# Heads paired four apart, whole batches of k and v in one tile, and chunks 6 to 11 worked by halves of 64 tokens

## The chip, the cores and the metric

The kernel runs on one core of one Trainium2 chip. The metric is the device time of one execution in microseconds. Before the change three runs gave 214.65, 214.87 and 215.19 us, a median of 214.87. One execution was profiled; it took 214.73 us.

## What is computed

A retention layer and a feed-forward layer, in float32 at the interface and bf16 on the way:

```python
gamma = 1 - 2.0 ** (-5 - h)                      # one per head h
state = gamma * state + outer(k[t], v[t])        # per batch and head, 64 x 64
y[t]  = q[t] @ state / sqrt(64)
x     = y, heads side by side: (4 * 768, 8 * 64)
out   = relu(x @ w_in) ** 2 @ w_out              # 512 -> 2048 -> 512
```

There are 4 batches, 8 heads, 768 tokens each, heads of 64. q, k and v are 6.3 MB each, w_in and w_out 4.2 MB each, the output 6.3 MB.

## The kernel before

**Chunks.** Tokens are taken in 24 chunks of 128 (six to a batch). Within a chunk the recurrence is a masked product: scores k q, times powers of gamma that are put into q and k beforehand, times a mask, times v; the state of the chunks before comes in as one more product. Chunks 0 to 3 (`PAIRED`) are worked two at a time by functions named `..._pair`. Chunks 4 to 11 go 128 tokens at a time with `attend`: `scale_q`, `scale_kv`, a transpose of q and k (on TensorE for chunks 4 to 7, by DMA from chunk 8 on, `DMA_FROM`), `scores`, `state`, `outputs`. Chunks 12 to 23 (`PACK_FROM`) go with `attend2` by two halves of 64 tokens: `scale_k2`, `cast_v2`, `transpose_k2` (by DMA), `scores2`, `state2` for each half, `outputs2`. In that form two heads share the 128 rows of a weight load, one on rows 0 to 63 and one on rows 64 to 127, which is why `cast_v2` writes a block-diagonal copy of v beside the plain one.

**Feed-forward.** `BLOCKS` puts four chunks into the first token block and two into each of the other ten. `ffn_pieces` cuts a block's two products into pieces of about 0.87 us of TensorE, eight to a chunk. After every piece a counter `n` goes up by one and `before(n)` issues what `put(place, ...)` has hung on that place: loads, scalings, transposes, scores, outputs. So all order is written by hand in places; place 32 is the end of the first block, and each later block has sixteen. Each engine works off its own instructions in that order.

**Heads and rows.** Heads 2p and 2p+1 make pair p; the 512 columns of x are in the order of the heads, and w_in is loaded in that order: 128 rows by 4 blocks.

**Loads.** All transfers are issued by SP, on one queue: loads, output stores and the transposes by DMA. Each waits until the transfer eight before it has landed, and, where its tile is used again, for those who read it. Weights are staged in a ring of five tiles of 1 MB, then cast to bf16 (`cast_w`, `cast_w_out`). k and v come by chunk (`load`) for chunks 4 to 11, in loads of 256 KB. For chunks 12 to 23 they come by threes (`group_loads`): per head one load of 96 KB into 64 rows, so sixteen loads for three chunks of k and v.

The lines of the profile are: L777 first product, L835 second product, L786 relu, L757 square, L367 and L380 transposes of q and k on TensorE, L421, L447, L476 and L484 scores, state and the two kinds of output matmuls of `attend`, L681, L708, L730 and L737 the same of `attend2`, L717 and L718 copies of the state, L744 the copy of the outputs, L353 `scale_kv`'s cast of v, L656 and L659 `cast_v2`, L643 `scale_k2`, L334 `scale_q`, L847 the stores.

Of the kernel before, what the change touches and what calls it, by code (L numbers as in the profile page):

```python
# [9 lines left out]
FP32 = mybir.dt.float32  # L10
# [9 lines left out]
LDBUFS = 4  # L20
# [4 lines left out]
DMA_FROM = 8  # L25


PACK_FROM = 12

GROUP = 3  # L30
# [3 lines left out]
def kernel(  # L34
# [9 lines left out]
    nc = tc.nc  # L44
# [22 lines left out]
    ldpool = ctx.enter_context(tc.tile_pool(name="ldpool", bufs=LDBUFS // 2))  # L67
    grpool = ctx.enter_context(tc.tile_pool(name="grpool", bufs=2))
    qspool = ctx.enter_context(tc.tile_pool(name="qspool", bufs=2))
    kspool = ctx.enter_context(tc.tile_pool(name="kspool", bufs=4))  # L70
# [6 lines left out]
    wstage = ctx.enter_context(tc.tile_pool(name="wstage", bufs=5))  # L77
# [43 lines left out]
    def group_loads(m):  # L121

        b, i = chunks[m]
        for name, src, to in (("kg", k, raw_k), ("vg", v, raw_v)):
            t = grpool.tile([P, 2 * GROUP, NPAIR, D], FP32, name=name)
            for h in range(H):
                p, hh = divmod(h, 2)
                rows = slice(64 * hh, 64 * (hh + 1))
                nc.sync.dma_start(
                    t[rows, :, p, :],  # L130
                    src[b, h, i * C : (i + GROUP) * C, :].rearrange("(w s) d -> s w d", s=64),
                )
                yield
            for j in range(GROUP):
                to[m + j] = t[:, 2 * j : 2 * j + 2].rearrange("s u p d -> s (u p) d")

    w_in_v = moe_w_in.rearrange("(cb p) f -> p cb f", p=P)
# [3 lines left out]
    def load_w_in(g, parts=1):  # L141
        t = wstage.tile([P, NCB, FQ], FP32, name="w_stage")
        n = FQ // parts
        for j in range(parts):
            nc.sync.dma_start(
                t[:, :, j * n : (j + 1) * n], w_in_v[:, :, g * FQ + j * n : g * FQ + (j + 1) * n]
            )
        staged["in", g] = t

    def load_w_out(g):  # L150
        t = wstage.tile([P, FPQ, DM], FP32, name="w_stage")
        nc.sync.dma_start(t[:], w_out_v[:, g * FPQ : (g + 1) * FPQ, :])
        staged["out", g] = t
# [16 lines left out]
    halves = [slice(0, 64), slice(64, 128)]  # L170
# [66 lines left out]
    def pack_constants():  # L237
        lng2 = const.tile([P, 2, NPAIR], FP32)
        for hh, rows in enumerate(halves):
            for p in range(NPAIR):  # L240
                nc.gpsimd.memset(lng2[rows, :, p : p + 1], float(np.log(gammas[2 * p + hh])))
        logs = lng2.rearrange("s u p -> s (u p)")
        ex = exponents([[C, NCH], [C // 2, 2], [0, NPAIR]], 1, "ex_k2", logs, halves)
        nc.scalar.activation(kf2.rearrange("s i u p -> s i (u p)"), ex[:], AF.Exp, scale=-1.0)
        nc.gpsimd.memset(cmask2[:], 0.0)
        for rows in halves:
            nc.gpsimd.affine_select(
                out=cmask2[rows],
                in_=cmask2[rows],
                compare_op=ALU.is_gt,  # L250
                fill=1.0,
                base=0,
                pattern=[[-1, 2], [-2, C // 4]],
                channel_multiplier=1,
            )
# [75 lines left out]
    def scale_q(m):  # L331
        b, i = chunks[m]
        qs = qspool.tile([P, 2, H, D], BF16, name="qs")
        nc.vector.tensor_tensor(  # L334
            out=qs[:],
            in0=raw_q.pop(m).rearrange("s h r d -> s r h d"),
            in1=qf[:, i : i + 2, :, None].to_broadcast([P, 2, H, D]),
            op=ALU.mult,
        )
        at[m]["qs"] = qs  # L340

    def scale_kv(m):
        b, i = chunks[m]
        ks = kspool.tile([P, H, D], BF16, name="ks")
        nc.vector.tensor_tensor(
            out=ks[:],
            in0=raw_k.pop(m)[:],
            in1=kf[:, i, :, None].to_broadcast([P, H, D]),
            op=ALU.mult,
        )  # L350
        v_bd = v_bds[m % 2]
        vn = raw_v.pop(m)
        nc.gpsimd.tensor_copy(  # L353
            v_bd[:, :, ::3, :], vn.rearrange("s (p hh) d -> s p hh d", hh=2)
        )
        at[m].update(ks=ks, v_bd=v_bd)
# [40 lines left out]

    def dma_transpose_k(m):
        a = at[m]
        kT = kTpool.tile([P, 2 * NPAIR, C], BF16, name="kT")  # L400
        nc.sync.dma_start_transpose(kT[:, 0:NPAIR], a["ks"].rearrange("s h d -> s (h d)"))
        a["kT"] = kT

    def spread_k(m):
        a = at[m]
        kT = a.pop("kT")
        k_bd = k_bds[m % 2]
        for hh in range(2):
            rows = slice(64 * hh, 64 * (hh + 1))
            nc.vector.tensor_copy(k_bd[rows, :, hh, :], kT[rows, 0:NPAIR])  # L410
        a["k_bd"] = k_bd
# [91 lines left out]
    def scale_pair_q(m, r, engine=nc.vector):  # L503
        b, i = chunks[m]
        if r == 0:
            at[m]["qs"] = qspool.tile([P, 2, H, D], BF16, name="qs")
        engine.tensor_tensor(
            out=at[m]["qs"][:, r],
            in0=raw_q[m].rearrange("s h r d -> s r h d")[:, r],
            in1=qf[:, i + r, :, None].to_broadcast([P, H, D]),  # L510
            op=ALU.mult,
        )

    def scale_pair_k(m, r):
        b, i = chunks[m]
        at[m]["ks"] = pair_view(ks_bd2s[m // 2])
        nc.vector.tensor_tensor(
            out=at[m]["ks"][:, r],
            in0=raw_k[m][:, r],
            in1=kfp[:, i + r, :, None].to_broadcast([P, H, D]),  # L520
            op=ALU.mult,
        )
# [54 lines left out]
    def state_pair(m, j):  # L577
# [5 lines left out]
        for p in range(NPAIR):  # L583
            for r in range(2):
                nc.tensor.matmul(  # L585
                    c[:, p],
                    lhsT=a["ks"][halves[j], r, 2 * p : 2 * p + 2, :],
                    rhs=a["v"][halves[j], r, 2 * p : 2 * p + 2, :],
                    start=(i + j == 0 and p == 0 and r == 0),
                    stop=True,  # L590
                    skip_group_check=True,
                )
# [4 lines left out]
    def outputs_pair(m, r, pools=None):  # L597
# [4 lines left out]
        for p in range(NPAIR):  # L602
            for hh, head in enumerate(halves):
                for j, rows in enumerate(halves):
                    nc.tensor.matmul(
                        a["y"][j][head, p, :],
                        lhsT=a["v"][rows, r, 2 * p + hh, :],
# [30 lines left out]
    def scale_k2(m):  # L638
# [3 lines left out]
        for hh, rows in enumerate(halves):  # L642
            nc.vector.tensor_tensor(  # L643
                out=ks[rows, :, hh, :],
                in0=kn[rows],
                in1=kf2[rows, i].rearrange("s u p -> s (u p)")[:, :, None].to_broadcast(
                    [64, 2 * NPAIR, D]
                ),
# [4 lines left out]
    def cast_v2(m):  # L653
        vn = raw_v.pop(m)
        v2 = v2pool.tile([P, 2 * NPAIR, D], BF16, name="v2")
        nc.gpsimd.tensor_copy(v2[:], vn[:])  # L656
        v_bd = v_bd2s[m % 2]
        for hh, rows in enumerate(halves):
            nc.gpsimd.tensor_copy(v_bd[rows, :, hh, :], vn[rows])  # L659
# [211 lines left out]
    scale_pair_q(0, 0)  # L871
    scale_pair_q(0, 1)
# [8 lines left out]
    scale_pair_q(2, 0, nc.gpsimd)  # L881
    scale_pair_q(2, 1, nc.gpsimd)
# [50 lines left out]
    def attend_q(m, scaled, transposed):  # L933
        if m % 2 == 0:
            put(scaled, scale_q, m)
            put(transposed, dma_transpose_q if m >= DMA_FROM else transpose_q, m)

# [3 lines left out]
    def attend(m, scaled, places):  # L941
        by_dma = m >= DMA_FROM
        attend_q(m, scaled, scaled if by_dma else places[0])
        put(places[0], scale_kv, m)
        if by_dma:
            put(places[0], dma_transpose_k, m)
        put(places[1], spread_k if by_dma else transpose_k, m)
# [5 lines left out]
    def attend2(m, d):  # L953
        attend_q(m, d - 17, d - 15)
        put(d - 15, scale_k2, m)
        put(d - 15, cast_v2, m)
        put(d - 13, transpose_k2, m)
        put(d - 6, state2, m, 0)
# [6 lines left out]
    for m, place in ((5, 10), (6, 14), (7, 18)):  # L965
        put(place, load, m)
# [7 lines left out]
    attend(6, 30, (33, 35, 37, 39, 42))  # L974
    attend(7, None, (40, 42, 44, 46, 49))
    put(50, pack_constants)
    for j, t in enumerate([s_bds[2]] + ks_bd2s + v_bd2s):
        for hh in range(2):
            put(51 + 3 * j + hh, zero_off_diagonal, t, hh)


    done = [55, 62, 70] + [78 + 8 * j for j in range(13)]
    for m, place in ((8, 29), (9, 31), (10, 36)):
        put(place, load, m)
    for m, d in zip(range(8, NCHUNK), done):
        if m < PACK_FROM:
            attend(m, d - 15 if d < 70 else d - 16, (d - 13, d - 7, d - 5, d - 3, d))
        else:
            attend2(m, d)
        if m + 3 < PACK_FROM:  # L990
            put(d - 13, load, m + 3)
        elif m + 3 < NCHUNK and (m + 3) % 2 == 0:
            put(d - 13, load_q, m + 3)
    for m, place in zip(range(PACK_FROM, NCHUNK, GROUP), (43, 67, 92, 116)):
        loads = group_loads(m)
        for j in range(2 * H):
            put(place + 3 * j // 2, next, loads)
        put(place + 3 * H, next, loads, None)
# [43 lines left out]
```

## Time and profile before

| what | value |
|---|---|
| median of three runs | 214.87 us |
| profiled execution | 214.73 us |
| its span, first to last instruction | 212.9 us |
| TensorE busy | 204.5 us, 96% |
| VectorE, ScalarE, POOL busy | 61%, 55%, 24% |
| bytes moved | 39.65 MB, mean 186 GB/s |
| SP's queue, share of 16 transfer engines | 79.4% |
| granted TensorE clock, mean | 0.992 |

The page divides the span into 40 slices and gives the busy share of each engine in tenths for each. The chain follows the work that ended last back to the start: who held up whom. In a table of stretches, the numbers behind an engine's name are its busy time and instructions in that stretch; the last three columns are the granted TensorE clock, the busy share of the sixteen transfer engines (it can pass 1, because transfers overlap) and the bytes moved per time. Times of SP's instructions are the time that SP spent on issuing; it grows where the queue is full.

### The profile page before, as it was taken

To read this page: it belongs to the slowest core of one execution; us is meant where nothing else is said; L and a number is where in the kernel's file an instruction comes from. 1 tells how busy PE (TensorE), PEld (TensorE's weight loads), DVE (VectorE), ACT (ScalarE), POOL (GpSimd) and SP (SyncE) were. 2 spreads that over 40 slices of the span, in tenths; PEclk is the share of its full clock that TensorE was granted. 3 is DMA by queue.
4 is the path that set the end of the run, shared out by engine and by line. 5 is a ranking of instruction groups with operands and counts; after the bars stand their busy time and mean duration, and the time that the engine had idled before them with its cause. 6 is when DMAs were issued, how large, how long until landed. Compare 5 with 4: busy or idle time off the path is not lost.

```text
span 212.9 us, 5128 instructions
## 1 busy us (share of the span) xinstructions
PE 204.5 (96%) x2077; PEld 142.1 (67%) x2077; DVE 129.4 (61%) x257; ACT 116.2 (55%) x216; POOL 50.6 (24%) x106
## 2 busy tenths in 40 slices
PE   5789999999999999999999999999999999999994
PEld 1467644558966975875875875875965965965853
DVE  4777875265585696796495595593694693640410
ACT  8365885358853643652663663652753754643631
POOL 5332466221110411025121323008122223000000
PEclk9889999999999999999999999999999999999999
DMA  6999999999969898599698698998795452401102
GB/s 162 290 317 383 386 386 258 293 242 274 276 172 201 199 197 145 161 207 182 164 197 191 154 189 188 152 194 202 164 240 127 99 80 72 102 0 49 52 0 99
DMA packets 90551, 39.65 MB, mean 186 GB/s; under 512 B 66336, under 2 KB 84000, under 8 KB 90528
## 3 DMA queue, kind: packets, MB, share of 16 engines
q1 hardware_dynamic: 90528, 39.33, 79.4%
q8 instruction: 16, 0.26, 0.6%
q14 instruction: 7, 0.06, 0.1%
HBM read 27.26 MB, written 6.29 MB: 158 GB/s over the span
## 4 chain that ended last, share of the span: by engine, by line
PE 90%; ACT 2%; DVE 2%; DMA 2%; POOL 1%; issue 1%; POOLq 0%; ACTq 0%; DVEq 0%
PE psf L835 38%; PE psf L777 38%; DMA qn<-in_q_dram 2%; PE st L421 2%; PE y L484 1%; PE st L681 1%; PE y L737 1%; PE y L730 1%; PE c_ps L708 1%; PE y L313 1%; DVE pt L568 1%; PE c_ps L585 1%; PE psf L544 1%; ACT osb L845 1%; PE c_ps L447 1%
## 5 line engine op out<-in xcount | busy, mean ns | idle before, releaser
L777 PE MATMUL psf<-xt,w_in_bf 128*128 128x256 bf16 (+2 forms) x880 | 90.7, 259 | 0.2 <-ACT xt L492 0.2
L835 PE MATMUL psf<-w_out_bf,h 128*128 128x512 bf16 (+2 forms) x400 | 89.6, 371 | 0.0
L777 PEld LDWEIGHTS <-w_in_bf 128*128 128x128 bf16 x880 | 71.3, 98 | 11.8 <-issue 0.3
L786 ACT ACTIVATE h<-psf 128x512 bf16<-128x512 f32 x96 | 57.0, 597 | 22.2 <-PE psf L777 19.6
L835 PEld LDWEIGHTS <-h 128*128 128x128 bf16 x400 | 36.3, 98 | 35.1
L757 DVE TENSOR_TENSOR h<-h 128x512 bf16<-128x512 bf16 x96 | 43.1, 467 | 21.0 <-ACT h L786 20.2
L845 ACT ACTIVATE osb<-psf 128x512 f32<-128x512 f32 (+2 forms) x25 | 14.5, 580 | 28.6 <-PE psf L835 28.6
L718 DVE CAST s_bd<-c_ps 64x256 bf16<-64x256 f32 x22 | 9.4, 427 | 27.4 <-ACT s_bd L717 27.1
L656 POOL CAST v<-vg 128x512 bf16<-128x512 f32 x12 | 8.1, 674 | 56.3 <-PE c_ps L708 21.0
L659 POOL CAST v_bd<-vg 64x512 bf16<-64x512 f32 x24 | 16.4, 682 | 15.0 <-PE y L737 14.1
L428 DVE TENSOR_TENSOR pt<-st,cmask 128x512 bf16<-128x512 f32 x16 | 11.1, 692 | 12.5 <-PE st L421 12.3
L643 DVE TENSOR_TENSOR ks_bdp<-kg,kf 64x512 bf16<-64x512 f32 x24 | 18.3, 762 | 0.4
L353 POOL CAST v_bd<-vn 128x512 bf16<-128x512 f32 x8 | 5.7, 718 | 36.2 <-PE y L484 29.1
L744 ACT ACTIVATE xt<-y 128x512 bf16<-128x512 f32 x12 | 8.9, 742 | 9.6 <-PE y L737 9.6
L334 DVE TENSOR_TENSOR qs<-qn,qf 128x1024 bf16<-128x1024 f32 x10 | 12.1, 1213 | 2.1 <-DMA qn<-in_q_dram 2.0
L717 ACT ACTIVATE s_bd<-c_ps 64x256 bf16<-64x256 f32 x22 | 8.1, 367 | 8.8 <-PE c_ps L708 8.8
L301 POOL CAST w_out_bf<-w_stage 128x512 bf16<-128x512 f32 x12 | 7.8, 689 | 5.5 <-DMA w_stage<-in_moe_w_out_dram 5.5
L492 ACT ACTIVATE xt<-y 128x512 bf16<-128x512 f32 x8 | 6.0, 749 | 5.5 <-PE y L484 5.2
L688 DVE TENSOR_TENSOR pt<-st,cmask 128x512 bf16<-128x512 f32 x12 | 8.3, 691 | 0.4
L313 PE MATMUL y<-ident 128*128 128x512 bf16 (+1 forms) x13 | 5.8, 558 | 2.1 <-POOL ident L199 2.1
L708 PEld LDWEIGHTS <-ks_bdp 128*128 128x128 bf16 x88 | 5.6, 98 | 2.6
L737 PE MATMUL y<-pt,v_bd 128*128 128x64 bf16 x96 | 7.0, 193 | 0.0
(99 smaller groups left out, 167.1 us busy)
## 6 DMA issues: line engine op xcount, KB each, us to landing
qn<-in_q_dram SPq DMA_DIRECT2D x12, 512.0 KB, 4.9
out_dram<-osb SPq DMA_DIRECT2D x23, 256.0 KB, 2.5
w_stage<-in_moe_w_out_dram SPq DMA_DIRECT2D x4, 1024.0 KB, 12.2
w_stage<-in_moe_w_in_dram SPq DMA_DIRECT2D x3, 1024.0 KB, 11.8
kg<-in_k_dram SPq DMA_DIRECT2D x32, 96.0 KB, 3.6
vg<-in_v_dram SPq DMA_DIRECT2D x32, 96.0 KB, 3.4
kn<-in_k_dram SPq DMA_DIRECT2D x8, 256.0 KB, 5.6
vn<-in_v_dram SPq DMA_DIRECT2D x8, 256.0 KB, 5.6
```

Of the source, the lines that this page charges most:

```text
L334: nc.vector.tensor_tensor(out=qs[:], in0=raw_q.pop(m).rearrange("s h r d -> s r h d"), in1=qf[:, i : i + 2, :, None].to_broadcast([P, 2, H ...
L428: nc.vector.tensor_tensor(out=a["pt"][:, 2 * half : 2 * half + 2], in0=st[:], in1=cmask.rearrange("s r t -> s (r t)")[:, None, None, :].to ...
L643: nc.vector.tensor_tensor(out=ks[rows, :, hh, :], in0=kn[rows], in1=kf2[rows, i].rearrange("s u p -> s (u p)")[:, :, None].to_broadcast([6 ...
L659: nc.gpsimd.tensor_copy(v_bd[rows, :, hh, :], vn[rows])
L718: nc.vector.tensor_copy(s_bd[halves[1], :, 1, :], c[halves[1]])
L737: nc.tensor.matmul(yv, lhsT=a["v_bd"][:, u * NPAIR + p], rhs=a["pt"][:, u * NPAIR + p, :].rearrange("s (r t) -> s r t", r=2), start=not inter,
L744: nc.scalar.activation(xts[tb][:, :, off : off + C].rearrange("e p (s r) -> e p r s", r=2), y[:], AF.Copy,)
L757: nc.vector.tensor_mul(hv, hv, hv)
L777: nc.tensor.matmul(hp, lhsT=w_in_bf[g][:, cb, fq * 128 : (fq + 1) * 128], rhs=xts[tb][:, cb, cols], start=(cb == 0), stop=(cb == NCB - 1),)
L786: nc.scalar.activation(hv, hp[:], AF.Relu)
L835: nc.tensor.matmul(op[:], lhsT=h_of(tb, f)[:, 0, j * C : (j + 1) * C], rhs=w_out_bf[g][:, fq, cols], start=(f == 0), stop=(f == NFB - 1),)
L845: nc.scalar.activation(osb[:, cols], op[:], AF.Copy)
```

## The change

1. **Pairing.** Pair p is now heads p and p + 4. Scalings go through one helper, `scale`, that reads in the loaded order and writes in pair order; `cast_v2`, `scale_k2` and the products of the paired chunks take the heads accordingly. Rows of w_in are in pair order, and each `load_w_in` is cut into one load per pair. `scale_q` becomes two instructions of one token parity each.
2. **Staging.** One ring of four tiles of 1.5 MB (`stage`) holds weights and whole batches of k or v, in place of the ring of five and the tiles of `group_loads`.
3. **Whole loads.** `load_batch` loads k or v of a whole batch with two loads of 786 KB into 64 rows each: for chunks 8, 12 and 18. The first of them is of batch 1, so it holds chunks 6 and 7 too, which are not taken from it.
4. **Own loads.** k and v of chunks 6 and 7 come by `load_two`, eight loads of 64 KB each, hung on places 13 to 18.
5. **Halves from chunk 6 on.** `PACK_FROM` goes from 12 to 6, so chunks 6 to 11 go with `attend2`, with outputs at places 47, 52, 59, 63, 70, 78 (before: 42, 49, 55, 62, 70, 78). q of chunk 6 and k of 6 and 7 are now transposed by DMA; k transposes of 8 to 11 grow to two halves. Constants and cleared blocks for the halves are made at places 14 to 24 instead of 50 to 64.

On SP the order is now: the first six loads, 20 loads of w_in, w_out 0 to 2, chunk 4, w_out 3, chunk 5, q of 6, the sixteen own loads, the first block's stores with q of 8 among them, the transposes of q and k of 6, k of batch 1, the transpose of k of 7, v of batch 1, q of 10, the transpose of q of 8, two stores, the transposes of k of 8 and 9. w_out 0 takes the tile of w_in 0, so it waits for the casts of that; before it had a tile of its own.

```diff
-PACK_FROM = 12
+PACK_FROM = 6
-    kspool = ctx.enter_context(tc.tile_pool(name="kspool", bufs=4))
+    kspool = ctx.enter_context(tc.tile_pool(name="kspool", bufs=2))
-    wstage = ctx.enter_context(tc.tile_pool(name="wstage", bufs=5))
+    stage = ctx.enter_context(tc.tile_pool(name="stage", bufs=4))
...
+    def load_two(m, name):
+        b, i = chunks[m]
+        src, to = (k, raw_k) if name == "k" else (v, raw_v)
+        t = ldpool.tile([P, 2 * H * D], FP32, name=name + "n")
+        t = t.rearrange("s (w p d) -> s w p d", w=4, p=NPAIR)
+        for w in range(4):
+            t0 = i * C + w * 64
+            for hh, rows in enumerate(halves):
+                nc.sync.dma_start(t[rows, w],
+                    src[b, NPAIR * hh : NPAIR * (hh + 1), t0 : t0 + 64].rearrange("p s d -> s p d"))
+                yield
...
+    def load_batch(m, name):
...
+        for hh, rows in enumerate(halves):
+            nc.sync.dma_start(
+                t[rows].rearrange("s p w d -> s (p w) d"),
+                src[b, NPAIR * hh : NPAIR * (hh + 1)].rearrange("p (w s) d -> s (p w) d", s=64),
+            )
...
-    w_in_v = moe_w_in.rearrange("(cb p) f -> p cb f", p=P)
+    w_in_v = moe_w_in.rearrange("(hh p d) f -> p hh d f", hh=2, d=D)
...
-            nc.sync.dma_start(
-                t[:, :, j * n : (j + 1) * n], w_in_v[:, :, g * FQ + j * n : g * FQ + (j + 1) * n]
-            )
+            for p in range(NPAIR):
+                nc.sync.dma_start(
+                    t[:, p, j * n : (j + 1) * n],
+                    w_in_v[p, :, :, g * FQ + j * n : g * FQ + (j + 1) * n],
+                )
...
+    def scale(engine, out, by, table):
+        engine.tensor_tensor(
+            out=out.rearrange("s (p hh) d -> s hh p d", hh=2),
+            in0=by.rearrange("s (hh p) d -> s hh p d", hh=2),
+            in1=table.rearrange("s (hh p) -> s hh p", hh=2)[:, :, :, None].to_broadcast([P, 2, NPAIR, D]),
+            op=ALU.mult,
+        )
...
-    for m, place in ((5, 10), (6, 14), (7, 18)):
-        put(place, load, m)
+    put(10, load, 5)
+    put(13, load_q, 6)
+    for name, place in (("k", 13), ("v", 16)):
+        loads = load_two(6, name)
+        for j in range(9):
+            put(place + j // 3, next, loads, None)
...
-    attend(6, 30, (33, 35, 37, 39, 42))
-    attend(7, None, (40, 42, 44, 46, 49))
-    put(50, pack_constants)
+    put(14, pack_constants)
...
+    done = [47, 52, 59, 63] + [70 + 8 * j for j in range(14)]
+    ahead = {6: (34, 35, 39), 7: (37, 38, 44), 8: (48, 49, 50), 9: (53, 54, 55), 10: (60, 61, 60)}
+    for m, d in zip(range(PACK_FROM, NCHUNK), done):
+        attend2(m, d, done[m - PACK_FROM - 1] if m > PACK_FROM else 0,
+                d - 17 if m < 8 else d - 18, *ahead.get(m, (d - 15, d - 13, d - 15)))
+    for m, name, place in (
+        (8, "k", 36), (8, "v", 39), (12, "k", 62), (12, "v", 66), (18, "k", 98), (18, "v", 106)
+    ):
+        put(place, load_batch, m, name)
```

`attend2` now takes the places of the scaling and the transpose of k and of the cast of v (the three numbers in `ahead`) as arguments.

## The prediction

> **What bounds the kernel now.** I read the page's first four parts, then stretches of the trace, then SP's issues in order of time.
>
> ```profile
> span 212.9 us, 5128 instructions
> PE 204.5 (96%) x2077; PEld 142.1 (67%) x2077; DVE 129.4 (61%) x257; ACT 116.2 (55%) x216; POOL 50.6 (24%) x106
> PE   5789999999999999999999999999999999999994
> DMA  6999999999969898599698698998795452401102
> PE 90%; ACT 2%; DVE 2%; DMA 2%; POOL 1%; issue 1%; POOLq 0%; ACTq 0%; DVEq 0%
> ```
>
> TensorE holds the chain: 90% of it, busy in every slice after the third. What idles it is the start; later only 0.27 us at 72 to 74. But the transfer engines are full from the second slice to the eleventh and are never far from it until the thirtieth. So TensorE's work sets the time only as long as the queue delivers in time, and the queue has little to spare.
>
> How fast it delivers, by stretches (the last two columns are the busy share of 16 transfer engines and GB/s):
>
> ```profile
> 8.00:12.00 4.00, 3.77 (x48) 2.23 (x47) 3.13 (x7) 1.75 (x3) 2.04 (x2) 0.58 1.22 290
> 14.00:17.00 3.00, 2.71 (x61) 2.05 (x62) 1.55 (x4) 2.58 (x6) 1.91 (x4) 1.00 1.11 360
> 22.00:29.00 7.00, 7.00 (x48) 3.68 (x46) 5.87 (x19) 5.45 (x12) 2.71 (x7) 1.00 1.05 386
> 45.80:49.00 3.20, 3.20 (x30) 1.98 (x28) 2.33 (x3) 2.72 (x6) 0.29 (x1) 1.00 1.35 221
> ```
>
> Rows of 512 bytes go at 290 GB/s, of 1 KB at 360, of 2 KB at 386, of 256 bytes (k and v) at 221. All sixteen engines share each load here: per engine 22.5 GB/s for 1 KB rows (360/16) and 24.1 for 2 KB (386/16).
>
> When SP issued (start, us spent):
>
> ```profile
> 6.68 1.74 SPq L102 DMA_DIRECT2D vn<-in_v_dram  x1
> 8.46 5.78 SPq L145 DMA_DIRECT2D w_stage<-in_moe_w_in_dram  x5
> 38.00 3.38 SPq L94 DMA_DIRECT2D qn<-in_q_dram  x1
> 45.34 1.01 SPq L113 DMA_DIRECT2D vn<-in_v_dram  x1
> ```
>
> Landings keep the order of issue throughout. The vn issued at 6.68 takes 7.3 us and lands at 14.0; the last w_in load, issued at 13.15, takes 13.3 and lands at 26.5; the vn of chunk 7 (45.34) takes 4.9 and lands at 50.2.
>
> **What it removes.** From the chain in order of time:
>
> ```profile
> 39.45 0.45 PE tp L367 x8
> 41.62 0.22 PE tp L380 x4
> 45.52 0.22 PE st L421 x4
> 45.74 0.22 PE c_ps L447 x4
> 101.93 0.12 PE c_ps L708 x4
> 102.92 0.23 PE st L681 x8
> ```
>
> A chunk of the old kind costs 2 x 0.22 (scores), 0.22 (state) and twelve output matmuls, 53.21 to 53.88, 0.67: 1.33. By halves: 0.23, 2 x 0.12 and sixteen output matmuls, 115.21 to 115.68, 0.47: 0.94. Four chunks save 0.39 each; chunk 6 (first of its batch) and chunk 11 (last) 0.3 each. Three transposes leave TensorE: q of chunk 6 (0.45), k of 6 and 7 (0.22 each). With the 0.27 us wait behind the constants, which are now made earlier, TensorE is relieved of 1.56 + 0.6 + 0.89 + 0.27 = 3.3 us.
>
> **New order on TensorE.** Chunk 7's outputs move to place 52, and the next piece reads them through ACT: 0.74 (L744) plus handover, 0.9 us idle (0.7 to 1.3). State of chunk 9 is formed twice with one piece between; its two copies (0.37 and 0.43) just fill that: 0.3 (0 to 1).
>
> **Costed at nothing.** VectorE: the split q scaling (two of 0.69 for one of 1.21, ten pairs, 1.7 us) and the clearing and constants moved to places 14 to 24 lie in its idle 39%. POOL: the casts of six more chunks (three of 0.68 in place of one of 0.72) lie in its idle 76%; without that cover each would delay an output by 1.3 us. The w_out 0 load now waits on SP for the casts of w_in 0, with w_out 1, w_out 2 and chunk 4 behind it. Before, w_out 1 waited for the same casts and went at 19.2, while the queue was full until 26.5: 0.
>
> **The queue past chunk 6.** SP is free at 41.4 (38.00 + 3.38). The sixteen own loads of k and v of 6 and 7 have 64 rows like the kg loads, which take 0.62 us of SP each: 51.3, the last landing 2.6 later, 53.9 (50.2 if SP needs 0.37 each, as for kn). Behind them in order: four stores of 0.68 (256 KB at 386), q of 8 (1.8), two transposes at 1.1 (in a full queue a kT lands 0.9 to 1.4 after what is ahead of it): 60.6. Then k of the whole batch, two loads of together 1.57 MB at 221: 7.1; kT of 7: 68.8. Then v: 75.9; q of 10, qT of 8, two stores, kT of 8: 81.3. Chunks 6 and 7 are in those whole loads a second time.
>
> TensorE, without any wait, is at place 40 at 59.40 - 0.67 = 58.7; with pieces of 0.87, the attention between them and the 0.9 above, it wants kT of 8 at place 54, at 73.5. So 7.8 us late (3 with rows at 272 GB/s, the stretch 56 to 57, and quick issues; 10 at 195, the stretch 156.5 to 158). The second batch (places 62 and 66, wanted at 80) comes out 0.8 late by the same sum (0 to 2.7).
>
> **How w_in is cut.** Its rows are now paired by heads four apart, so each load is cut in four, and its source is walked as 2 x 64 rows with a jump between, its destination as 128. Every load in the trace of before has the same outermost count on both sides, 128 or 64, and keeps all sixteen engines busy. No row shows sides that disagree. If engines are dealt equal shares of the outermost step of both sides, 2 against 128 leaves two engines. The ends: sixteen engines, 0 us; two engines, 1.05 MB of 1 KB rows at 45 GB/s, 23.3 us, and 3.15 MB of 2 KB rows at 48.2, 65.2: 14.0 + 88.5 = 102.5 in place of 26.5, **76 us** later, with every later load behind it on these two. I take the two: sharing by the outermost step is the one description that fits all loads shown, and here it can give no more.
>
> The Trainium skill's page "DMA: Bandwidth & Descriptors" (section "Why a DMA increments its semaphore by 16 and not by 1") states this as a rule: the largest number up to 16 that divides the slowest dimension of both sides. By it the sum is the two-engine one; without it, the sixteen-engine one. The trace agrees for 128 and 64; that two are used is shown by no run here.
>
> Sum, against the profiled run's own 214.73 us (span 212.9 and 1.8 around it; 0.14 under the median): -3.3 + 0.9 + 0.3 + 7.8 + 0.8 = +6.5, then +76, since kT of 8 sits in the same queue: 297.
>
> **Rivals.**
> 1. Sixteen engines carry w_in, the queue is late at chunks 7 and 8: 214.7 + 6.5 = 221 (216 to 225 by the ends). For it: 386 GB/s for every w load so far; against it: no load so far had unequal sides.
> 2. The faster side: sixteen engines, and kT of 8 lands by place 54. Then 214.7 - 3.3 + 1.2 = 212.6. It decides at 2.1 us: if kT of 8 lands before 75.6, the kernel gains. For it: SP's short issues (0.37) and stretches above 270 GB/s; against it: ten queue items worth 20.7 us between 60.6 and 81.3.
> 3. In between, kT of 8 2 us late: 214.7, no change.
>
> **How the numbers follow.** Two engines 0.82, rival 1 0.13, rival 2 0.03, rival 3 0.02. Within the first, 284 (engines a few per cent quicker when fourteen are idle, nothing late afterwards: 88.5 becomes 84, 6.5 becomes -2) to 308 (w_in 6 us slower, transposes and batch loads at the slow ends). That range holds nearly all of the 0.82, so 0.8. A change under 0.3% (0.6 us) could not be told from none here: faster 0.03, same 0.02, slower 0.95.
>
> **What would show it.** Two engines: w_in landing some 76 us later, the busy share of the transfer engines near 2/16 and about 48 GB/s from 14 to 100 us, TensorE idle three times in turn, until about 59, 81 and 103, behind casts that wait for the stage tiles of w_in 1, 2 and 3; after that st waiting for kT at chunks 7 and 8. Rival 1: 386 GB/s at 22 to 29 and TensorE idle near 68 and 78 only. TensorE's busy time falls by 3.1 in each case; xt of chunk 7 holds it 0.9. I am wrong if w_in loads run at over 100 GB/s.

## The result, and the profile after

The changed kernel takes 329.16 us (median of 4 runs, 328.41 to 330.48), the kernel before 214.89 beside it: ratio 1.532, 95% interval 1.527 to 1.538. It is 114.3 us slower. The forecast was 297, so its direction and its main cause hold, and 32 us are missing from it. The profiled run took 328.41 us, with a span of 326.3. Some single runs come out about 2% longer at a lower granted clock, and the times in this document leave them out: one of f1's two below (238.9, the one that was profiled, against 234.4) and one of h2's four (228.1).

The page after, in the parts that were read before (busy time; the span in 40 slices, with the granted clock as PEclk; the chain by engine):

```profile
span 326.3 us, 5158 instructions
PE 225.0 (69%) x2087; PEld 149.3 (46%) x2109; DVE 131.3 (40%) x265; ACT 115.0 (35%) x217; POOL 57.3 (18%) x118
PE   6914520603313999667578936999980999999996
PEclk9967575655755999985979979999998799999999
DMA  8811111111179495999963999769999628245001
PE 44%; SPq 27%; DMA 23%; DVE 2%; ACT 1%; issue 1%; POOL 0%; POOLq 0%; ACTq 0%
```

TensorE held 90% of the chain and now holds 44%. Two stretches are to be seen. From slice 3 to slice 11 the transfer engines are busy to one tenth, and TensorE mostly idles. From slice 17 on the transfer engines are at 9 again, and TensorE still has holes. The row PEclk shows that TensorE is not only idle in these holes: its granted clock is down.

The first stretch (the last three columns are granted clock, busy share of the 16 transfer engines and GB/s), and the chain of waits to its end:

```profile
14.00:40.00 26.00, 10.31 (x146) 7.84 (x144) 4.49 (x10) 5.59 (x13) 2.77 (x6) 0.65 0.14 47
40.00:60.00 20.00, 5.33 (x36) 3.50 (x35) 2.76 (x9) 2.17 (x4) 1.49 (x4) 0.59 0.13 50
```

```profile
59.46 5.15 SPq L165
64.66 5.15 SPq L165
69.85 5.15 SPq L165
78.74 23.99 DMA stage<-in_moe_w_in_dram
102.78 0.41 POOL w_in_bf L311
```

The share is near 2/16 (0.125), the rate 47 to 50 GB/s, and each quarter of a load takes 5.15 us. The last w_in load lands at 78.74 + 23.99 = 102.7, where the forecast had 102.5. The second block's first piece starts at 124.55 (49.86 before): 74.7 us late.

So 114.3 - 74.7 = 39.6 us are lost behind that point, where the forecast had 6.5. The waits of TensorE, and its costliest group (busy us, mean ns, idle time before it):

```profile
PE st L671 <- DMA kT<-ks_bdp: 26.4, 7, 7.9
PE c_ps L698 <- POOL v L644: 3.2, 2, 2.6
L767 PE MATMUL psf<-xt,w_in_bf 128*128 128x256 bf16 (+2 forms) x879 | 106.1, 281 | 62.9 <-POOL w_in_bf L311 31.3 <-ACT w_in_bf L315 15.5 <-DVE w_in_bf L313 15.1
```

Seven scores wait for a kT, in three batches, and not only chunks 7 and 8. The first product of the feed-forward part, the same matmuls as before, is busy for 106.1 us (90.7 before).

### The profile page after: what moved, and what is told of

Its sections match the earlier page's. It is cut to its first block, busy times and chain, and to the rows that moved or that the text cites. A ratio compares the mean times of both kernels' runs of the same rounds, so it can differ in the third digit from the quotient of the medians.

```text
span 326.3 us, 5158 instructions
## 1 busy us (share of the span) xinstructions
PE 225.0 (69%) x2087; PEld 149.3 (46%) x2109; DVE 131.3 (40%) x265; ACT 115.0 (35%) x217; POOL 57.3 (18%) x118
## 4 chain that ended last, share of the span: by engine, by line
PE 44%; SPq 27%; DMA 23%; DVE 2%; ACT 1%; issue 1%; POOL 0%; POOLq 0%; ACTq 0%
SPq L165 21%; PE psf L825 21%; PE psf L767 18%; DMA stage<-in_moe_w_in_dram 7%; DMA stage<-in_v_dram 7%; DMA qn<-in_q_dram 5%; DMA kT<-ks_bdp 4%; SPq L99 2%; SPq L148 1%; SPq L655 1%; PE st L671 1%; SPq L837 1%; PE c_ps L698 1%; PE y L727 1%; PE y L720 1%
## 5 line engine op out<-in xcount | busy, mean ns | idle before, releaser
L767 PE MATMUL psf<-xt,w_in_bf 128*128 128x256 bf16 (+2 forms) x879 | 106.1, 281 | 62.9 <-POOL w_in_bf L311 31.3
L767 PEld LDWEIGHTS <-w_in_bf 128*128 128x128 bf16 x880 | 78.4, 107 | 83.1 <-POOL w_in_bf L311 28.6
L708 DVE CAST s_bd<-c_ps 64x256 bf16<-64x256 f32 x33 | 14.1, 428 | 49.1 <-ACT s_bd L707 48.6
L647 POOL CAST v_bd<-stage 64x512 bf16<-64x512 f32 x32 | 21.6, 674 | 31.5 <-PE y L727 30.6
L644 POOL CAST v<-stage 128x512 bf16<-128x512 f32 x16 | 9.8, 613 | 97.8 <-DMA stage<-in_v_dram 66.7
L671 PE MATMUL st<-qT,kT 128*128 128x64 bf16 x144 | 8.0, 204 | 26.4 <-DMA kT<-ks_bdp 26.4
L633 DVE TENSOR_TENSOR ks_bdp<-stage,kf 64x512 bf16<-64x512 f32 x32 | 22.7, 710 | 4.3 <-DMA stage<-in_k_dram 3.7
L671 PEld LDWEIGHTS <-kT 128*128 128x128 bf16 x144 | 6.7, 104 | 30.3 <-DMA kT<-ks_bdp 28.7
L678 DVE TENSOR_TENSOR pt<-st,cmask 128x512 bf16<-128x512 f32 x18 | 12.5, 692 | 18.2 <-PE st L671 17.9
L353 DVE TENSOR_TENSOR qs<-qn,qf 128x512 bf16<-128x512 f32 x22 | 15.3, 708 | 6.5 <-DMA qn<-in_q_dram 6.4
L698 PE MATMUL c_ps<-v,ks_bdp 128*128 128x64 bf16 x132 | 9.5, 196 | 3.7 <-POOL v L644 3.2
```

What stands on the lines that cost most here:

```text
L353: engine.tensor_tensor(out=out.rearrange("s (p hh) d -> s hh p d", hh=2), in0=by.rearrange("s (hh p) d -> s hh p d", hh=2), in1=table.rear ...
L633: nc.vector.tensor_tensor(out=ks[rows, :, hh, :].rearrange("s (u p) d -> s u p d", u=2), in0=kn[rows], in1=kf2[rows, i, :, :, None].to_bro ...
L647: nc.gpsimd.tensor_copy(v_bd[rows, :, hh, :].rearrange("s (u p) d -> s u p d", u=2), vn[rows])
L671: nc.tensor.matmul(st[:, c, :], lhsT=kT[:, c, :], rhs=half_of(a["qT"], p, u), start=True, stop=True,)
L698: nc.tensor.matmul(c[:, p, :], lhsT=a["ks"][:, u * NPAIR + p], rhs=a["v2"][:, u * NPAIR + p, :], start=(i == 0 and u == 0 and p == 0), sto ...
L708: nc.vector.tensor_copy(s_bd[halves[1], :, 1, :], c[halves[1]])
```

## Experiments

Two questions are open: whether two engines are what made w_in slow, and where the 39.6 us come from, of which 33 were not forecast. Theory A: they belong to the loads past chunk 6. Theory B: late weights press everything behind them together. All times below are medians; the kernel before ran beside each and gave 214.4 to 214.9. Most of these runs load other rows than the kernel needs, or in another order, and so measure time alone; e1, h2 and h3 compute the layer itself.

### e1, e2, e3: the loads of w_in alone

e1 is the changed kernel with this edit:

```diff
-            for p in range(NPAIR):
-                nc.sync.dma_start(
-                    t[:, p, j * n : (j + 1) * n],
-                    w_in_v[p, :, :, g * FQ + j * n : g * FQ + (j + 1) * n],
-                )
+            for hh, rows in enumerate(halves):
+                nc.sync.dma_start(
+                    t[rows, :, j * n : (j + 1) * n],
+                    w_in_v[:, hh, :, g * FQ + j * n : g * FQ + (j + 1) * n].rearrange(
+                        "p d f -> d p f"
+                    ),
+                )
```

> The changed kernel, but each part of w_in is loaded as two loads of 64 rows (head halves) instead of four loads of 2 x 64 rows: the same bytes in the same tile, both sides now walked as 64. Both theories: w_in runs at 350 to 390 GB/s and has landed by 28 us. Theory A (the part of the loss that the forecast missed comes from the whole loads themselves, 1.57 MB each at about 150 GB/s with the kT transposes behind them, whatever w_in does): 329 - 76 = 253 us (245 to 258), with TensorE waiting for kT and v of chunks 6 to 8, 12 and 18. Theory B (the missed part comes from w_in being late, which presses all later loads together): 221 us (216 to 225), with a wait of about 8 us in the first batch and about 1 us in the later ones.

e2 is the kernel before with the changed kernel's loop over p and its source, 2 x 64 rows:

```diff
-    w_in_v = moe_w_in.rearrange("(cb p) f -> p cb f", p=P)
+    w_in_v = moe_w_in.rearrange("(hh p d) f -> p hh d f", hh=2, d=D)
```

and e3 has the same loop with a source of 4 x 32 rows:

```diff
-    w_in_v = moe_w_in.rearrange("(cb p) f -> p cb f", p=P)
+    w_in_v = moe_w_in.rearrange("(a p d) f -> p a d f", a=4, d=32)
```

> The kernel before, with w_in alone loaded as in the changed kernel, four loads of 2 x 64 rows for each part; its rows are thereby paired for another order of heads, which this kernel does not have, so its products are others. Two engines: share 2/16 and 48 GB/s from 14 to about 102 us, time 214.9 + 76 = 291 us (287 to 296). If it comes out well above (over 300), lateness of w_in costs more than its own length, and part of the loss that the forecast missed belongs to it. If it stays under 225, the count of engines was not what made w_in slow.

> As the run before, but the source of each w_in load is walked as 4 x 32 rows with jumps (128 on the other side; other rows than the kernel needs, the same bytes). If engines are dealt by the outermost step of both sides: four engines, share 4/16, 90 to 96 GB/s, w_in landing at 14.0 + 11.7 + 32.6 = 58.3 us instead of 26.5, time 239 to 247 us. If any mismatch of the two sides falls to two engines: 291 us. If it is the jump alone that costs: 214.9 to 220 us.

Measured: e1 263.59 us (ratio 1.226, 1.222 to 1.229), e2 289.94 (1.350, 1.347 to 1.352), e3 249.02 (one run). The stretch of 14 to 40 us in e2 and e3, and 16 to 28 in e1:

```profile
14.00:40.00 26.00, 10.72 (x146) 8.22 (x147) 4.72 (x10) 6.00 (x14) 2.89 (x6) 0.67 0.14 47
```

```profile
14.00:40.00 26.00, 16.57 (x184) 11.60 (x186) 7.57 (x20) 8.59 (x17) 4.26 (x10) 0.74 0.27 97
```

```profile
16.00:28.00 12.00, 8.05 (x125) 6.04 (x124) 5.85 (x14) 5.92 (x13) 3.40 (x8) 1.00 1.10 215
```

Two steps outside give a share of 0.14 and 47 GB/s, four give 0.27 and 97. Divided by two and by four that is 23.5 and 24.3 GB/s for one engine, where 386/16 is 24.1: the number of engines follows the outermost step. (The views give the mean of all sixteen, so the number is read from share and rate.) e2 loses 75.1 us, nearly the forecast's 76, with nothing else of the change in it. e3's w_in lands at 61.5 (58.3 expected), and its 249 is 2 us above its range.

e1 has sixteen engines and still loads w_in at 215 GB/s, not at the 350 to 390 that I expected: 64 rows on each side, share 1.10. That makes its weights late by 8 to 9 us (the second block starts at 58.16). What is lost behind that point is 48.8 - 8.3 = 40.5. Theory B's 221 is far off; theory A's range (to 258) missed by 5.6 us, since it had not those 8.

### f0: the rest of the change alone

The changed kernel with the w_in load of the kernel before:

```diff
-            for p in range(NPAIR):
-                nc.sync.dma_start(
-                    t[:, p, j * n : (j + 1) * n],
-                    w_in_v[p, :, :, g * FQ + j * n : g * FQ + (j + 1) * n],
-                )
+            nc.sync.dma_start(
+                t[:, :, j * n : (j + 1) * n], w_in_v[:, :, g * FQ + j * n : g * FQ + (j + 1) * n]
+            )
```

> The changed kernel, with w_in loaded exactly as in the kernel before (128 rows on both sides; these rows are paired for the old order of heads, so the products are others). It leaves the rest of the change alone in the time. In the run with 64-row loads the first piece of the second block started at 58.16, 8.3 us after its time before (49.86), and the end came 48.7 us late: so 40.4 lie behind that point; in the changed kernel it is 114.3 - 74.7 = 39.6. Theory A (the missed loss belongs to the loads past chunk 6): 214.9 + 40 = 255 us (250 to 258). If part of it belonged to late weights: under 245. The forecast's own sum: 221.

Measured 254.83 (1.184, 1.178 to 1.190): 40.2 us lost with w_in in time. 75.1 (e2) and 40.2 add up to 115.3; measured together were 114.3. Theory A holds, and the two losses add. f0 is the base of the runs below. SP's issues in it, answering to those shown before (start, us spent):

```profile
54.51 0.54 SPq L835 DMA_DIRECT2D out_dram<-osb  x1
59.88 2.05 SPq L653 DMA_TRANSPOSE kT<-ks_bdp  x1
62.02 3.54 SPq L148 DMA_DIRECT2D stage<-in_k_dram  x2
65.66 7.38 SPq L653 DMA_TRANSPOSE kT<-ks_bdp  x1
73.14 3.48 SPq L148 DMA_DIRECT2D stage<-in_v_dram  x2
86.35 2.50 SPq L653 DMA_TRANSPOSE kT<-ks_bdp  x1
```

and what the chain of waits has of them:

```profile
59.88 4.13 DMA kT<-ks_bdp
73.79 11.82 DMA stage<-in_v_dram
86.35 5.65 DMA kT<-ks_bdp
```

kT of chunk 6 lands at 64.0, v of the batch at 85.6, kT of chunk 8 at 92.0. TensorE's waits for them:

```profile
PE st L669 <- DMA kT<-ks_bdp: 27.8, 7, 6.2
PE c_ps L696 <- POOL v L642: 3.9, 2, 2.3
```

It waits 27.8 us for kT and 3.9 for v: 14.8 in the first batch (3.5 at chunk 6, 6.2 at 7, 5.1 at 8), 8.0 in the second, 8.8 in the third.

### f1, f3: rows, and blocks

f1 makes each whole load one of 128 rows:

```diff
-        for hh, rows in enumerate(halves):
-            nc.sync.dma_start(
-                t[rows].rearrange("s p w d -> s (p w) d"),
-                src[b, NPAIR * hh : NPAIR * (hh + 1)].rearrange("p (w s) d -> s (p w) d", s=64),
-            )
+        nc.sync.dma_start(
+            t.rearrange("s p w d -> s (p w) d"), src[b].rearrange("h (w s) d -> s (h w) d", s=P)
+        )
```

f3 keeps the 64 rows and cuts by head, a piece or two to a place:

```diff
         for hh, rows in enumerate(halves):
-            nc.sync.dma_start(
...
+            for p in range(NPAIR):
+                nc.sync.dma_start(
+                    t[rows, p], src[b, NPAIR * hh + p].rearrange("(w s) d -> s w d", s=64)
+                )
+                yield
...
-        (8, "k", 36), (8, "v", 39), (12, "k", 62), (12, "v", 66), (18, "k", 98), (18, "v", 106)
+        (8, "k", 36), (8, "v", 40), (12, "k", 58), (12, "v", 62), (18, "k", 86), (18, "v", 98)
```

> As f0, but each whole load of k or v is one load of 128 rows x 48 pieces of 256 bytes instead of two of 64 rows x 48: the same bytes, the same size of piece, tokens in other rows than the kernel needs. Theory A1 (the whole loads are slow because 64 rows go at 157 GB/s, 5.0 us for 786 KB, and at 221 GB/s the forecast would have held): a whole tensor takes 7.1 us in place of 10.2, the waits for kT shrink from 26 us to under 8, time 217 to 229. Theory A2 (pieces of 256 bytes, 16 KB apart, are slow for any number of rows): 10 us each, time as f0, 250 to 258.

> As f0, but each whole load of 64 rows is cut into one load for each head (64 rows x 12 pieces, 197 KB), issued one or two to a place over 4 to 11 places, from place 36, 40, 58, 62, 86 and 98: same bytes, same 64 rows. If the loss comes from a transpose that has to wait behind a block of 10 us, a transpose now waits behind 1.3 to 3 us: waits for kT fall below 10 us in all, time 218 to 235. If the loss is the queue's whole throughput (it can't carry these bytes in the time at 64 rows), the waits move to k and v but the time stays: 247 to 258.

Measured: f1 234.4 (one run; its profile is of the other, at 238.9), f3 239.8 (ratio 1.118, 1.115 to 1.120), between its two ranges. While whole loads run, f0 in two stretches:

```profile
65.00:74.00 9.00, 4.37 (x38) 2.23 (x36) 1.72 (x4) 1.81 (x4) 0.00 (x0) 0.93 1.42 158
76.00:85.00 9.00, 7.99 (x108) 6.67 (x106) 3.59 (x7) 4.00 (x8) 0.00 (x0) 0.80 1.37 156
```

and f1 in two:

```profile
65.00:73.00 8.00, 5.60 (x39) 2.60 (x37) 1.74 (x4) 1.81 (x4) 0.00 (x0) 0.89 1.19 195
75.00:81.00 6.00, 5.89 (x88) 4.97 (x87) 3.25 (x7) 3.19 (x7) 0.00 (x0) 0.83 1.13 221
```

The same bytes in the same 256-byte pieces go at 156 to 158 GB/s into 64 rows and at 195 to 221 into 128: by these rates a tensor takes about 10 us or 7 to 8. That is A1's mechanism, and 20 us of time. But f1 stays above A1's range, with 17.7 us of waits for kT in its profile: loads near the 7.1 us that my forecast had would not have given its 221 either. f3 shows the other part. It leaves the rate and takes the blocks: waits for kT fall from 27.8 to 9.6, as expected, but in the first batch 10.6 us of waiting for v come in their place, so that batch waits 14.1 us in all (f0: 14.8). Behind 100 us it waits 6.1 in all (f0: 16.8). There, as the edit shows, the loads also start 4 to 12 places sooner than in f0; no run parts the cutting from the sooner start, so the 15 us belong to both together.

### g2: a queue of its own for the whole loads

In the loop of the whole loads, on top of f0:

```diff
-            nc.sync.dma_start(
+            nc.scalar.dma_start(
                 t[rows].rearrange("s p w d -> s (p w) d"),
```

> As f0 (254.8), but the whole loads are issued by ScalarE on a queue of its own, so that no transpose stands behind them on SP's queue; same bytes, same 64 rows, same places. If position in one queue is what makes kT late: waits for kT below 8 us in all (27.8 in f0), time 230 to 243, the rest of the loss being k and v of the first batch. If the sixteen engines' throughput is what makes it late: waits as before, 250 to 258. ScalarE spends about 3.5 us on issuing for each tensor, which may cost up to 5 us of it.

Measured 249.1 (248.3 to 250.0): between its two ranges. Waits of TensorE:

```profile
PE psf L823 <- ACT h L774: 10.1, 1, 10.1
PE st L669 <- DMA kT<-ks_bdp: 7.3, 4, 2.7
PE c_ps L696 <- DVE s_bd L706: 7.1, 4, 5.3
```

The waits for kT fall as the position in the queue says (27.8 to 7.3), but ScalarE stands in its issues instead (5.68 us for one of them, in the chain at 73.30), with its relu and the copies of the state behind them. Part of the wait was moved, not removed. The run tells that position matters, and not how much time it is worth.

### g3, g4, g5, h1: the causes together

g3 has rows and pieces together, at f3's places. g4 and g5 leave out the second read of chunks 6 and 7, g4 with 128 rows and g5 with 64. The pieces of g4 (in g3, n is 6):

```diff
+        n = NCH - i
+        for h in range(H):
+            nc.sync.dma_start(
+                t[:, h // 2, 2 * i + h % 2 * n : 2 * i + (h % 2 + 1) * n],
+                src[b, h, (NCH - n) * C :].rearrange("(w s) d -> s w d", s=P),
+            )
+            yield
```

h1 is g4 with the own loads of chunks 6 and 7 in 128 rows:

```diff
-        for w in range(4):
...
+        for j in range(2):
+            nc.sync.dma_start(
+                t[:, 2 * j : 2 * j + 2].rearrange("s w p d -> s (w p) d"),
+                src[b, :, (i + j) * C : (i + j + 1) * C].rearrange("h s d -> s h d"),
+            )
+            yield
```

> As f0, with both remedies together: each whole tensor as eight loads by head, 128 rows x 6 pieces (197 KB), at the places of f3; tokens in other rows than the kernel needs. Theory: rate (64 rows) and block (transposes behind 10 us) are two separate causes, and what is left after both is the first batch, whose bytes come too late: 227 to 232 (236.7 by the rows alone, 239.8 by the pieces alone). If rate and block are the same cause seen twice: 235 to 240.

> As f3 (239.8: pieces of 64 rows), without the second read of chunks 6 and 7. The second read is 1.05 MB at 157 GB/s, 6.7 us of the queue ahead of k and v of chunk 8: the wait for v in the first batch (10.6) falls to about 4, time 230 to 235. If the queue has slack there after all, no change: 238 to 241.

> As g3, and the first batch's loads leave out chunks 6 and 7, which are loaded on their own anyway: 131 KB for each head instead of 197, 1.05 MB less in all. Theory of three causes (64 rows, blocks, second read): with all three gone the change costs what the forecast's other terms say, 213 to 220, with under 5 us of waits for k, v and kT. If it stays above 225, there is a cause that I have not named.

> As g4 (227.3), and the own loads of k and v of chunks 6 and 7 are four loads of 128 rows (262 KB) in place of sixteen of 64 rows (65 KB); tokens in other rows than the kernel needs. In g4 these sixteen hold SP for 12 us (43 to 55) while the transfer engines are half idle, and kT of chunk 6 lands at 65.7, 4.9 us late. If that is the fourth cause: SP is free 7 to 9 us sooner, kT of chunk 6 is in time, the waits for kT and v fall from 9.8 to under 3 us, time 213 to 219. If the queue's throughput sets this landing anyway: 225 to 228.

| run | rows of the whole loads | pieces | second read | own loads | us | waits for kT + v |
|---|---|---|---|---|---|---|
| f0 | 64 | no | yes | 16 of 64 rows | 254.8 | 27.8 + 3.9 |
| f1 | 128 | no | yes | same | 234.4 | 17.7 + 1.1 (at 238.9) |
| f3 | 64 | yes | yes | same | 239.8 | 9.6 + 10.6 |
| g5 | 64 | yes | no | same | 232.0 | 8.1 + 6.6 |
| g3 | 128 | yes | yes | same | 229.8 | 6.5 + 5.4 |
| g4 | 128 | yes | no | same | 227.3 | 7.4 + 2.4 |
| h1 | 128 | yes | no | 4 of 128 rows | 221.3 | 2.1 + 2.6 |

The times of g3 and g5 came out as expected; g5's wait for v fell to 6.6 us and not to 4. Rows and blocks (with the sooner start) are two causes that overlap: 20 and 15 us alone, 25 together. The second read is worth 7.8 us at 64 rows (f3 to g5). At 128 rows (g3 to g4) the medians differ by 2.5, which is not clear of noise: the intervals of their ratios are 1.052 to 1.088 and 1.050 to 1.067. g4 missed its range: there was a cause I had not named. SP's issues in g4 show it:

```profile
43.29 5.48 SPq L131 DMA_DIRECT2D kn<-in_k_dram  x8
48.81 6.17 SPq L131 DMA_DIRECT2D vn<-in_v_dram  x8
60.93 2.61 SPq L655 DMA_TRANSPOSE kT<-ks_bdp  x1
```

and in h1, where kT of chunk 6 goes out 6.4 us sooner:

```profile
42.81 1.81 SPq L129 DMA_DIRECT2D kn<-in_k_dram  x2
44.66 2.66 SPq L129 DMA_DIRECT2D vn<-in_v_dram  x2
54.56 2.04 SPq L651 DMA_TRANSPOSE kT<-ks_bdp  x1
```

Sixteen short issues keep SP for 11.7 us, while the transfer engines' share is only 0.40 from 48 to 55 us in g4. With four issues of 4.5 us in all, the end comes 6 us sooner (227.3 to 221.3). h1 changes the rows of these loads as well as their number; the low share speaks for the number. h1 is still 6.4 above the kernel before (ratio 1.029, 1.024 to 1.033), 2.3 over its range: 4.7 us of waits are left.

### h2, h3: the halves with the loads of the kernel before

Can chunks 6 to 11 go by halves without the new pairing? h2 is the kernel before, with its loads by head in groups of three chunks from chunk 6 on, at the changed kernel's places; h3 asks for the transposes sooner:

```diff
-PACK_FROM = 12
+PACK_FROM = 6
...
+    for m, place, step in (
+        (6, 13, (1, 3)), (9, 31, (1, 1)), (12, 50, (1, 1)), (15, 67, (3, 2)),
+        (18, 92, (3, 2)), (21, 116, (3, 2)),
+    ):
+        loads = group_loads(m)
+        for j in range(2 * H):
+            put(place + step[0] * j // step[1], next, loads)
```

and from h2 to h3:

```diff
-    ahead = {6: (34, 35, 39), 7: (37, 38, 44), 8: (48, 49, 50), 9: (53, 54, 55), 10: (60, 61, 60)}
+    ahead = {6: (30, 31, 37), 7: (34, 35, 42), 8: (45, 46, 49), 9: (50, 51, 55), 10: (57, 58, 60)}
...
-                d - 17 if m < 8 else d - 18, *ahead.get(m, (d - 15, d - 13, d - 15)))
+                27 if m < 8 else d - 18, *ahead.get(m, (d - 15, d - 13, d - 15)))
```

> The kernel before (its pairing of heads, its w_in, its loads by head of 64 rows x 6 pieces, three chunks in one group) with chunks 6 to 11 by halves too, at the changed kernel's places; groups of chunks 6 and 9 issued from place 13 and 31. It computes what the reference does. No second read, no two engines, no blocks; left are the 64 rows at about 157 GB/s: 3.1 MB of chunks 6 to 11 in 20 us where the kernel before takes 14. If the queue can lend these 6 us: 214.6 - 3.3 + 1.2 = 212.5. If not, chunks 6 to 8 wait for them: 216 to 224.

> As h2 (223.25; it computes what the reference does), with the scaling and the transposes of chunks 6 to 10 at earlier places: q of 6 from place 27 instead of 30, k of chunk 6 scaled and transposed at 30 and 31 (34, 35), of 7 at 34, 35 (37, 38), of 8 at 45, 46 (48, 49), of 9 at 50, 51 (53, 54), of 10 at 57, 58 (60, 61). In h2 kT of chunk 6 is issued at 60.9, though its k landed at 49.8, and TensorE waits 6.8 us for kT four times. If the places were too late: the waits fall below 2 us, the clock stays up, and the halves give what the forecast said: 212.5 to 216. If the queue's throughput sets the landing of kT: waits of 5 us or more again, 220 to 224.

Measured: h2 222.82 (1.038, 1.034 to 1.043), h3 222.32 (1.036, 1.034 to 1.039). TensorE's waits, h2 in the first line, h3 in the other two:

```profile
PE st L681 <- DMA kT<-ks_bdp: 6.8, 4, 3.8
PE st L681 <- DMA kT<-ks_bdp: 5.4, 2, 4.2
PE tp L380 <- DVE ks L345: 1.5, 1, 1.5
```

Asking sooner moved the waits and hardly shortened them. At chunk 6 the places did matter: its kT goes out at 58.0 instead of 60.9, and TensorE waits 1.3 us instead of 3.8. But kT of chunk 8 lands at 79.8 instead of 80.4, behind pieces of the next groups that SP works off at 0.62 to 0.66 us each, and TensorE now waits 4.2 us for it (1.1 in h2). A new wait of 1.5 us stands at chunk 5, whose k VectorE scales only after the q of chunk 6, which lands late. So the places set the landing at chunk 6, and the queue sets it at chunk 8. No version of the halves that I ran beats the kernel before. In h2 SP issues almost without a pause from 41 to 61 us, the sixteen loads of the first group taking 11.0 us of it, while the transfer engines' share is 0.79 from 48 to 55: there it is SP's time that has no room.

## Why the prediction was wrong

**Right: w_in on two engines.** Share, rate, landing (102.7 against 102.5) and price (75.1 in e2 against 76) came as worked out. The Trainium skill's page "DMA: Bandwidth & Descriptors" (section "Why a DMA increments its semaphore by 16 and not by 1"), which the prediction weighed, is borne out by both points: 2 x 64 against 128 rows gave 47 GB/s and 4 x 32 gave 97. TensorE's waits behind the last parts of w_in 1, 2 and 3 ended at 58.2, 79.3 and 103.2 us (59, 81 and 103 forecast). One part of it was wrong: later loads were not all behind w_in on these two engines. From 80 to 100 us the share is 0.48 at 144 GB/s, so w_out moved beside the last of w_in.

**Failed: "The queue past chunk 6", with the second batch: 7.8 + 0.8 = 8.6 us.** Measured in f0: 31.7 us of waits. The mechanism (a late kT) was right; the size was off, by four things.
- The rate. I took 7.1 us for 1.57 MB "at 221 GB/s", a row of loads into 128 rows. The whole loads have 64, and a tensor took 10.0 to 10.6 us in f0. The range had 195 GB/s as its slow end; 157 lies outside it.
- kT of 6. I let the sixteen own loads end at 53.9 and kT of 6 land at 60.6, in time. In f0 the last own load landed at 56.2 and kT at 64.0: 3.5 us of waiting at a place where I had none. kT is 3.4 us behind its forecast, and 2.3 of them are the own loads; in h1, where four loads replace the sixteen, kT of 6 is in time.
- The later batches. I gave the second 0.8 and the third nothing, by asking when k and v are wanted, and not which kT stands behind them: a kT that goes out behind 10 us of load cannot make the eight places between its place and the scores (7 us at 0.87). Measured 8.0 and 8.8. Cut in pieces and started sooner (f3), both together wait 6.1.
- The slow end of the sum. It moved the first batch by 2.2 us (7.8 to 10) and the second by 1.9 (0.8 to 2.7); the third had no term.

**Failed: "TensorE's busy time falls by 3.1 in each case".** It rose from 204.5 to 225.0. The relief itself is there: in h2 the groups of matmuls and transposes of chunks 4 to 23 sum to 43.6 us against 47.1 before. TensorE's busy time as a whole shows none of it, even in h2 (205.2). The feed-forward products, the same matmuls, took 181.6 in h2, 188.6 in f0 and 198.8 in the changed kernel, against 180.3. Before and in f0:

```profile
L777 PE MATMUL psf<-xt,w_in_bf 128*128 128x256 bf16 (+2 forms) x880 | 90.7, 259 | 0.2 <-ACT xt L492 0.2
L835 PE MATMUL psf<-w_out_bf,h 128*128 128x512 bf16 (+2 forms) x400 | 89.6, 371 | 0.0
L823 PE MATMUL psf<-w_out_bf,h 128*128 128x512 bf16 (+2 forms) x400 | 94.8, 385 | 0.6 <-POOL w_out_bf L319 0.6
L765 PE MATMUL psf<-xt,w_in_bf 128*128 128x256 bf16 (+2 forms) x880 | 93.8, 266 | 1.0 <-ACT xt L732 0.8 <-ACT xt L496 0.2
```

After a wait the same piece can run slow, here right behind a wait at 137 us and far from one at 213, in the chain of the changed kernel:

```profile
137.61 3.11 PE psf L825 x8
213.06 1.73 PE psf L825 x8
```

It is not so after every wait. In f0, behind the waits for kT of chunks 6, 7 and 8, the clock (third number from the end) was 1.00, 0.55 and 0.50:

```profile
64.00:66.00 2.00, 1.94 (x16) 1.03 (x17) 1.29 (x2) 0.00 (x0) 0.00 (x0) 1.00 1.15 194
76.00:80.00 4.00, 4.00 (x35) 2.90 (x33) 1.97 (x3) 0.94 (x2) 0.00 (x0) 0.55 1.37 155
92.00:96.00 4.00, 3.95 (x43) 3.95 (x44) 2.56 (x6) 0.60 (x1) 0.00 (x0) 0.50 0.68 127
```

So waits cost more than their length: 8.3 us in f0 on top of 31.7. For f0 the terms close: 31.7 of waits for kT and v, 8.3 of slow products, 1.3 for xt and s_bd, 0.6 behind w_out casts, less about 3 of relief, is 39; 40.2 were measured. That the waits cause the slow clock is read from the rows and was not tried alone.

**Right: the small terms.** xt of chunk 7 held TensorE 0.8 (forecast 0.9), s_bd of chunk 9 0.5 (0.3). VectorE's and POOL's extra work held up nothing in f0. The w_out 0 load cost at most 0.6 (f0).

**The rivals.** Rival 1 (221) is f0 as I imagined it; f0 is 254.8. It shows that the same error sat in both, and only the share of w_in kept the forecast near.

The row-count error was readable. The Trainium skill's page "SBUF — State Buffer" (section "Door 1: The DMA port swizzle") says that 64 partitions reach only half of the ports, 218 GB/s at best; its section "Can I just issue two DMAs to hit both halves?" says that two such loads at once don't make up for it. The traces agree for w_in: 215 GB/s in 64 rows, the halves loaded in turn (e1), where 128 rows had 386. For 256-byte pieces they show less than the halving: 157 against 195 to 221.

Nor did every load of 64 rows go at 157, as the expectation of h2 had it. h2's loads of 96 KB, which go in turn to rows 0 to 63 and 64 to 127, moved 189 GB/s with the queue full, near the 195 of the same kind of load before (156.5 to 158):

```profile
46.00:49.70 3.70, 3.70 (x37) 2.39 (x35) 2.34 (x3) 3.15 (x7) 0.00 (x0) 1.00 1.27 189
```

f0's two large loads and f3's four pieces for one half stay in that half for longer. No run changes the order of the halves alone, so whether that order makes the difference stays open.

## What to carry to other kernels

Price a transfer by a row of the trace that has the same number of rows and the same outermost steps on both sides, not only the same piece size: here 386, 215, 97 and 47 GB/s were the same bytes of w_in. A load of 10 us in a queue delays every small transfer issued behind it, so ask of each batch what is queued behind it, for all batches and not the first alone. Count what SP spends on issuing too: a load of 64 rows kept it for about 0.6 us, whether of 64 KB (g4), 96 KB (h2) or 197 KB (f3). And where the engine that sets the end must wait, allow for what its clock may lose afterwards, in f0 a quarter of the waits' own length.

## What the runs showed of the hardware that I had not expected

- Loads of 64 rows show a full busy share of the sixteen transfer engines and still run slow: share 1.10 at 215 GB/s in e1, 1.42 at 158 GB/s in f0. A busy share near one is no sign of full rate.
- The two losses add almost exactly (75.1 + 40.2 against 114.3), although the first leaves TensorE idle for most of 75 us.
- Granted clock 0.59 for some 60 us of short work between waits, and 0.50 in the 4 us after the wait for kT of chunk 8 in f0 (92 to 96), but 1.00 after the 3.5 us at chunk 6.
- Left open: why 256-byte pieces in 64 rows get 157 in f0, and not 110, 215 or the 189 of h2; and q of chunk 8, 5.0 to 6.0 us from issue to landing in f0 and g4 with little ahead of it.
